# Two branches on one core: first projections in column halves, first weights in longer pieces, and a new order of all steps

## The chip, the cores and the metric

The kernel runs on one core of a Trainium2 chip. A core has a matrix engine (TensorE, in the profile PE, with its weight loads as PEld), VectorE (DVE), ScalarE (ACT), GpSimd (POOL) and SyncE (SP), which here only issues DMA transfers. They run side by side and wait for each other through semaphores. Matrix products land in PSUM, which the kernel uses as eight banks of 128 rows of 512 single-precision numbers. DVE and ACT evict them from there to SBUF, the working memory. The metric is the time of one execution in microseconds on the device; lower is better.

## The reference

Two independent branches read inputs of 2048 tokens by 448 and their outputs are put side by side. Branch A is attention with 16 heads of 28 over 8 keys at distances 0, 2, ... 14:

```python
qkv = x @ wqkv                                   # 448 -> 3 * 448
idx = pos[:, None] - off[None, :]                # off = 0, 2, ..., 14
logits = einsum("bhsd,bhswd->bhsw", q, k[idx]) * 28 ** -0.5
attn = softmax(where(idx >= 0, logits, -1e9))
a = einsum("bhsw,bhswd->bhsd", attn, v[idx]) @ wo
```

Branch B is a linear recurrence with 448 complex states:

```python
Lam_bar = exp(dt * Lam);  B_bar = ((Lam_bar - 1) / Lam)[:, None] * B
h[t] = Lam_bar * h[t - 1] + B_bar @ x[t]
y = 2 * real(C @ h) + x * Dskip
```

## The kernel before, in words

The whole kernel is written out by hand as a list of named steps, the string ORDER (lines 32 to 61). Each word names a function, its arguments as digits, the PSUM banks it takes after "@", and for an eviction the engine: "." is ACT, "=" is DVE. The loop at line 981 runs through the list, and every engine takes its own instructions in the order in which the list emits them. Waits between engines follow from the data. The transfers at lines 149 to 189 are issued ahead of the list, and SP takes them in that order too; what the list sends to SP comes behind them. POOL's constants (lines 193 to 238) are also ahead of the list.

The steps, in the order in which they matter:

- WU (22 products of zeros, L277) and WF (two each, L284) keep PE busy until data is there.
- XI, XH, XA transpose tokens of branch A on PE (L305 to L340); xi, xh, xa copy them from PSUM into xT, in four blocks of columns of x (the fourth, half as wide, comes by XI2 and XH). XI0 and XI1 take tokens 0 to 255 and 256 to 511. The second 1024 tokens are transposed by DMA (L183).
- QS (L374, L375) and QK (L259, the helper `part`) project to q and k for a block m of 128 columns; QK with k = 1 works on 64 rows, in pairs. qk and qh evict them. V_ and v do the same for the values.
- P (L405, DVE) multiplies q by shifted k, 24 of full rows and 4 of half heads, for the halves u = 0 and 1 of the tokens; the results lie in seven buffers used in turn. E_ (L417, L421) sums them over the 28 numbers of each head with products into two banks. lt and TD scale and transpose the scores; sma, smb, smc are the softmax.
- AL, al, ad, sp, AX, adx, spx bring the probabilities into banded form by way of memory (pd, pdx) into PT, 12 slots of a tile each, which pm0 to pm2 clear before on POOL; pm4 clears two of the buffers (Ak) that al2 and al3 fill, pm3 clears wo. AV and av multiply by the values, W_, w and ow are the output projection.
- PP, pcopy, pa to pg compute the constants of branch B; ty, tk, tf, ts make its rotation tables; rb makes small rotations R.
- LC loads C, ci and CD rearrange it, ca and cs scale it. BD and xt transpose B and x by DMA; LD loads Dskip, xd multiplies it.
- BU (L259) is B_bar x for group g of 64 states, BR (L761) adds the step before, z evicts; UP, y, sa, sb, sd, DN, dn carry the recurrence over blocks of four tokens. H_, h, sw, hp (ACT, L872, L874), hy and hz (DVE, L878, L883) bring the carried state back into Z. C, c, oc and, for the last, CH, ch, oh give the output.

xbuf holds x of branch A first, then the transposed x of branch B, then results, so its later uses wait for the earlier ones. The seven P buffers, Cn and Cr lie in memory that PT and wo take over later. The first four weight transfers (w_load at lines 155 and 156) fetch columns 0 to 255 of q and of k in two blocks of 128 columns each, in pieces of 256 bytes.

Of the kernel before, what the change touches and what calls it, by code (L numbers as in the profile page):

```python
# [29 lines left out]


ORDER = """
WU@0 XI0@1 WF0 xi00= xi01= XI2@2 PP@3 pcopy pa XI1@4 WF1 WF2 WF3 xi10. xi20= pb pd_ pc pe xi11. QS00@5 QS10@6 QS30@7
XH1@0 ty0 ty1 pf tk0= tk1= tf0 XA10@1 xh1= QS20@3 pg ab rb0 ts00 xa10. XA11@2 xa11. QK050@40 qk000. xt0 qk010. P000
qk020. QS11@1 qk011. P001 mz QS01@2 qk001. qk030. ts10 P010 ts20 ty4 QS21@5 QS31@6 qk031. qk021. QK041@31 tk4= QK051
P011 V_101@27 QK040 V_100 wj. QK060@65 ty5 qk041. qk040. qk051. v101. V_000@13 qk050. V_011@07 QK061 V_001 v100.
qh011. P020 E_00@42 v000. v001. P021 E_02 tk5= tf2 qh010. P030 qh001. qh000. E_01 P031 P040 P041 P050 P051 V_010
V_400@13 hc0 P060 v011. v010. QK110@56 ts02 ts12 V_401 QK101@70 QK111 E_03 P061 qk110. qk111. QK100 qk100. QK120@56
E_04 qk101. ts22 E_05 E_06 lt00 lt01 QK131@70 QK121 v401. qk120. TD0 QK130 qk130. v400. QK150@42 QK151 QK141@35
QK161@71 qk131. qk150. P100 P101 P110 qk121. qk151. E_10@03 P111 P120 QK140 qk141. P121 QK160 qk140. V_110@46 V_501@25  # L40
qh110. ty2 V_111 P130 P131 qh111. v110. qh101. qh100. v111. E_11 E_12 V_500 V_410@14 V_510@76 V_411 V_511 ty3 BD0 hc1
sma0 smb0 E_13 P140 v500. v501. P141 P150 P151 E_14 E_15 v511. v510. xt2 xt3 xt1 BU300@25 v410. v411. P160 P161 LC
E_16 lt11 BD1 lt10 TD1 smc0 OZ BU301 z30. ci1. LD BU001@67 BU101@14 BU000 ci3. z00. BR31 BU100 BU201@30 z10. AL0@2
al0. z31. BR01 ci0= CD3 CD0 z01. rb3 tk2= BU200 z20. BR11 z11. dk. ci2= CD2 BU011@61 CD1 OP pm3 AL1@2 BR21 BU010 BR02
sma1 z21. BU110@57 smb1 z02. ad0 tk3= tf1 ts01 al1= ad1 BU111 BR03 BR12 xd0 BU210@34 z03. pm4 smc1 BU311@02 z12. ts11
xd1 BU501@65 UP0 BU211 y0= pm0 BR13 BU310 ca3 ca6 z13= wo UP1 cs3 BR32 AX@1 y1= ax. BU500 xd2 ca1 cs6 BU400@71 z50.
ts21 BR51 BR22 AL2@6 BU401 z32. z22. sp0 BU601@03 BR33 sa0 BR23 al2. ty6 BU600 z33. cs1 UP3 z40. z51. sb0 AL3@6 tk6=
tf3 BR41 z23. UP2 BU511@75 z60. y3. BU510 BR61 BU411@02 sd0 y2= ca2 ca4 z41. z61. DN0@4 pm1 sp1 BU410 ts03 ad2 BR52
z52. adx BR42 ts13 z42. BR53 al3= ad3 z53. sa2 dn0 pm2 cs4 AV021@6 av021. AV000@1 AV031@4 AV030@3 UP5 sb2 sd2 av031.
BR43 z43. sp2 AV010@7 av010= y5= AV011@0 DN1@6 av030. dn1 av011. spx AV001@4 AV020@3 DN2@7 dn2 cs2 hp020 UP4 av020.  # L50
DN3@0 av000. BU610@56 dn3 BU611 BR62 W_10@7 W_20@3 y4= ca5 ca0 av001= z62. sa4 H_01@1 h01 sb4 W_00@0 W_01@2 H_00@4
hp012 BR63 W_11@5 hp011 w20. w01. ts23 w11. w10. w00. H_03@1 sd4 W_30@3 W_21@2 DN4@5 z63= hp010 h03 UP6 W_31@7 y6. dn4
hp022 h00 sa6 H_02@0 w21. DN5@1 sp3 AV120@5 av120. dn5 h02 AV111@6 av111. AV131@4 AV121@2 av121. av131. sw2 ow20
AV101@5 av101. AV100@1 H_04@6 cs5 AV130@0 H_05@2 av130. AV110@4 hp123 av110. av100. w30= W_61@3 W_71@5 hp113 cs0 sb6
sd6 C32@0 DN6@4 xd3 ow01 hp025 dn6 C33@1 ow11 sw0 hp111 sw4 hp115 hp122 hp112 ow00 H_06@4 h04 w31= ow31 w71= ow10 ow21
sw6 h05 hp023 hy2 h06 ow30 hp121 C30@6 C31@7 c30 hp021 hz2 hy1 W_51@5 c31 c32 hp124 c33 oc33 C00@2 hp125 C01@4 W_50@6
oc30 oc32 hp013 hy3 W_60@7 hp114 W_40@0 w61. hz1 hp110 hp120 hy0 hp015 hy5 w51. w50= hz5 hz0 hp024 hp014 hy4 C02@3
ow71 hp116 hz3 hz4 hp026 hp016 oc31 hp126 hy6 hz6 W_41@1 w41. w60. ow61 ow50 C03@5 c00 oc00 w40. W_70@6 C12@1 C10@7
C11@0 C13@2 c01 c02 c03 ow41 ow51 oc03 C21@4 oc02 ow40 oc01 w70. C20@6 ow70 c10 c11 c12 oc10 ow60 C22@3 oc11 CH0@5
CH1@7 oc12 c13 c20 c21 oc13 c22 ch0 ch1 oc20 oc21 oc22 oh0 oh1  # L60
"""

@with_exitstack
def kernel(
# [63 lines left out]
    def w_load(c, n, *at):  # L128

        for d in at:  # L130
            SP.dma_start(wq[:, 0:3, c + d:c + d + n], wq_r[:, :, c + d:c + d + n])
# [102 lines left out]
    kph = const.tile([128, 2, 5, G], F32, tag="kph")  # L234
    for k in range(5):
        POOL.memset(kph[:, 0, k], max(k, 1) / (2.0 * T))
    POOL.memset(kph[:, 1], 0.0)
    POOL.memset(kph[64:128, 1, 1:5], 0.25)
# [129 lines left out]
    @op  # L368
    def QS(m, s):

        p = ps()
        pp.setdefault(("qk", 0, m), {})[s] = p
        for kt in range(3):
            PE.matmul(p[:], wqk(m, slice(0, 128), kt), xT[:, 0, 4 * s + kt], start=(kt == 0), stop=False)  # L374
# [641 lines left out]
```

## Time and profile before

| | |
|---|---|
| median of 3 runs | 127.11 us (126.85 to 127.17) |
| the profiled execution | 127.13 us, span 125.4 us |
| busy: PE, DVE, ACT, POOL | 120.6, 113.6, 102.4, 22.7 us |
| instructions: PE, DVE, ACT | 1061, 211, 198 |
| moved by DMA | 22.34 MB, 57493 packets, 43943 of them under 512 B |

The span runs from the first to the last instruction in the trace; the time of the execution holds 1.7 us more that lie around it. Times in the trace are counted from the start of the span. Busy PE time counts overlapping matrix products once; one product of 512 columns lasts 380 ns by itself, but the next one starts about 215 ns after it. In lists by time, a row has its start, its length, engine, line, operation, output and inputs, sizes, the count of merged instructions, and in brackets the idle time of the engine before it with what ended it.

### The profile page before, as it was taken

Reading aid. Unit: us, or ns where it says so; the run is one execution under the profiler, and the core shown is the slowest. Engines: PE = TensorE matmul, PEld = TensorE weight load, DVE = VectorE, ACT = ScalarE, POOL = GpSimd, SP = SyncE. Lnnn points to the kernel's source line nnn. Section 1 sums busy time; section 2 is a strip of 40 time slices with the busy share of each in tenths; the row PEclk is TensorE's granted clock in tenths of the full one; section 3 lists DMA queues with packets and bytes.
Section 4 is the critical chain, followed back from the end, with each engine's and each line's share of the span. In section 5 each row is a group of like instructions: output and inputs, shape, how many; then the busy total and the mean of one; then the engine's idle time right before and its main releaser. Section 6 shows DMA issues by size and latency. Waiting matters only on the chain.

```text
span 125.4 us, 2898 instructions
## 1 busy us (share of the span) xinstructions
PE 120.6 (96%) x1061; PEld 59.0 (47%) x1061; DVE 113.6 (91%) x211; ACT 102.4 (82%) x198; POOL 22.7 (18%) x49
## 2 busy tenths in 40 slices
PE   6999999999999999999999998999999999999990
PEld 6835434443334343344344443745565555555560
DVE  4588999899999999999999999999999999998561
ACT  0599899897596999889999999999999999980000
POOL 6815400000000000090599900000000000000000
PEclk9999999999999999999999999999999999999999
DMA  3898998899969999858999999979854051334652
GB/s 97 208 278 204 325 251 181 191 194 253 157 143 213 204 204 224 144 127 188 358 221 129 160 154 400 156 100 160 177 130 120 0 169 54 124 103 141 227 180 74
DMA packets 57493, 22.34 MB, mean 178 GB/s; under 512 B 43943, under 2 KB 56935, under 8 KB 57479
## 3 DMA queue, kind: packets, MB, share of 16 engines
q1 hardware_dynamic: 57272, 22.08, 82.6%
q8 instruction: 8, 0.13, 0.5%
q10 hardware_dynamic: 207, 0.07, 0.3%
q14 instruction: 6, 0.05, 0.2%
HBM read 9.86 MB, written 6.37 MB: 129 GB/s over the span
## 4 chain that ended last, share of the span: by engine, by line
PE 77%; ACT 17%; DVE 2%; issue 2%; ACTq 0%; DVEq 0%
PE ps L259 27%; PE ps L897 16%; PE ps L573 10%; ACT Z L114 7%; ACT ctmp L722 5%; PE ps L417 5%; PE ps L374 4%; PE ps L560 4%; PE ps L277 2%; PE ps L827 1%; PE ps L375 1%; PE ps L922 1%; PE ps L761 1%; ACT L694 1%; PE ps L421 1%
## 5 line engine op out<-in xcount | busy, mean ns | idle before, releaser
L405 DVE TENSOR_TENSOR pr<-qf,kf 128x2048 bf16<-128x2048 bf16 x24 | 27.9, 1220 | 0.7 <-PE ps L417 0.4
L259 PE MATMUL ps<-xbuf,BT 128*128 128x512 bf16 (+1 forms) x112 | 25.1, 380 | 0.0
L897 PE MATMUL ps<-Cw,Z 128*128 128x448 bf16 x105 | 20.9, 352 | 0.0
L259 PE MATMUL ps<-xT,wq 128*128 128x512 bf16 (+1 forms) x72 | 16.0, 380 | 0.0
L259 PEld LDWEIGHTS <-BT 128*128 128x128 bf16 (+1 forms) x112 | 9.1, 96 | 12.9 <-issue 4.5
L897 PEld LDWEIGHTS <-Z 128*128 128x128 bf16 x105 | 10.3, 98 | 9.5 <-DVE Z L883 0.2
L114 ACT CAST Z<-ps 128x512 bf16<-128x512 f32 (+1 forms) x28 | 13.8, 547 | 0.2
L573 PE MATMUL ps<-wo,oT 128*128 128x448 bf16 x64 | 13.7, 353 | 0.0
L259 PE MATMUL ps<-wq,xT 128*128 128x448 bf16 (+1 forms) x64 | 12.3, 353 | 0.0
L973 POOL MEMSET PT<- 128x4320 f32 x3 | 11.0, 3698 | 4.7 <-DVE z L461 4.7
L259 PEld LDWEIGHTS <-wq 128*128 128x128 bf16 (+1 forms) x72 | 5.9, 97 | 8.6 <-issue 2.4
L722 ACT ACTIVATE ctmp<-Cw,c2t 64x448 f32<-64x448 bf16 x14 | 9.3, 666 | 0.2
L573 PEld LDWEIGHTS <-oT 128*128 128x128 bf16 x64 | 6.2, 98 | 5.7
L259 PEld LDWEIGHTS <-xT 128*128 128x128 bf16 (+1 forms) x64 | 5.2, 97 | 6.8 <-issue 2.4
L114 ACT CAST qf<-ps 128x512 bf16<-128x512 f32 x12 | 6.8, 594 | 1.8 <-PE ps L259 1.5
L114 ACT CAST oT<-ps 128x512 bf16<-128x512 f32 x15 | 8.1, 641 | 0.0
L114 ACT CAST v_s<-ps 128x448 bf16<-128x448 f32 x16 | 7.9, 548 | 0.0
L761 PE MATMUL ps<-Z,R 128*128 128x512 bf16 x21 | 7.3, 381 | 0.5 <-ACT Z L114 0.5
L114 ACT CAST kf<-ps 128x512 bf16<-128x512 f32 x12 | 7.1, 604 | 0.3 <-PE ps L375 0.2
L949 POOL MEMSET Z<- 128x14 bf16 x1 | 0.1, 111 | 38.9 <-ACT Cn L117 38.9
L374 PE MATMUL ps<-xT,wq 128*128 128x512 bf16 x24 | 6.6, 379 | 0.3 <-DVE u L627 0.2
L872 ACT ACTIVATE PT<-PT,bcol 128x512 bf16<-128x512 bf16 x8 | 6.3, 816 | 0.0
(172 smaller groups left out, 226.8 us busy)
## 6 DMA issues: line engine op xcount, KB each, us to landing
PT<-pd SPq DMA_DIRECT2D x16, 156.0 KB, 4.8
...
```

The lines of the kernel that those rows point to most:

```text
L114: (ACT.copy if e == "A" else V.tensor_copy)(o, i)
L259: PE.matmul(o, l, r, start=(first and i == 0), stop=(not first and i == len(pairs) - 1 and not more[s]))
L374: PE.matmul(p[:], wqk(m, slice(0, 128), kt), xT[:, 0, 4 * s + kt], start=(kt == 0), stop=False)
L405: V.tensor_tensor(t[:], q.unsqueeze(1).to_broadcast((128, 4, 512)), k4, ALU.mult)
L417: PE.matmul(acc[s][32 * i:32 * i + 32], E[:, f, ws, :], t[:, i, :], start=(f == 0 and ws == 0), stop=False)
L560: PE.matmul(p[32 * hh:32 * hh + 32, 128 * bl:128 * bl + n], v_s[:, t, 4 * hg + hh, :], PT[:, t % NS, (4 * hg + hh) // HS, (4 * hg + hh) % ...
L573: PE.matmul(p[:, 0:D], late["oT"][:, b // 4, hg, par, 128 * (b % 4):128 * (b % 4) + 128], late["wo"][:, hg, :], start=(hg == 0), stop=(hg ...
L722: ACT.activation(t[a:a + 64, 0:D], Cw[b:b + 64, g, :], ACTF.Copy, scale=c2t[a:a + 64, g:g + 1])
L761: PE.matmul(pp["z", g, j][:], rot(g, 0), late["Z"][:, g, j - 1, :], start=False, stop=True)
L872: ACT.activation(t, late["SW"][:, NC * g:NC * (g + 1)], ACTF.Copy, scale=bcol[:, j - 1, g:g + 1])
L897: PE.matmul(p[:, 0:D], z, Cw[:, g, :], start=(g == 0), stop=(g == G - 1))
L973: POOL.memset(late["PT"][:, 4 * i:4 * i + 4].rearrange("p t g n -> p (t g n)").bitcast(F32), 0.0)
```

## The change

1. The first four weight transfers become two: columns 0 to 255 of q and of k in one each, in pieces of 512 bytes.
2. A new step QA(m, a) projects block m for half a (256 columns of tokens) of the first 512 tokens. QA(0, 1), QA(0, 0), QA(1, 0) and QA(1, 1) take the place of QS00 and QS10.
3. On POOL, the constants kph are set before the halos and masks, and so is the row of numbers iota, which was set before them already and now follows kph.
4. WF4 is added: two more products of zeros.
5. All steps stand in a new order, with other banks; 18 evictions or table steps go from ACT to DVE and 22 from DVE to ACT. LC goes from behind the score steps to the start of the list, so its four loads are the first that the list sends to SP.

```diff
 ORDER = """
-WU@0 XI0@1 WF0 xi00= xi01= XI2@2 PP@3 pcopy pa XI1@4 WF1 WF2 WF3 xi10. xi20= pb pd_ pc pe xi11. QS00@5 QS10@6 QS30@7
-XH1@0 ty0 ty1 pf tk0= tk1= tf0 XA10@1 xh1= QS20@3 pg ab rb0 ts00 xa10. XA11@2 xa11. QK050@40 qk000. xt0 qk010. P000
-qk020. QS11@1 qk011. P001 mz QS01@2 qk001. qk030. ts10 P010 ts20 ty4 QS21@5 QS31@6 qk031. qk021. QK041@31 tk4= QK051
-P011 V_101@27 QK040 V_100 wj. QK060@65 ty5 qk041. qk040. qk051. v101. V_000@13 qk050. V_011@07 QK061 V_001 v100.
-qh011. P020 E_00@42 v000. v001. P021 E_02 tk5= tf2 qh010. P030 qh001. qh000. E_01 P031 P040 P041 P050 P051 V_010
-V_400@13 hc0 P060 v011. v010. QK110@56 ts02 ts12 V_401 QK101@70 QK111 E_03 P061 qk110. qk111. QK100 qk100. QK120@56
-E_04 qk101. ts22 E_05 E_06 lt00 lt01 QK131@70 QK121 v401. qk120. TD0 QK130 qk130. v400. QK150@42 QK151 QK141@35
-QK161@71 qk131. qk150. P100 P101 P110 qk121. qk151. E_10@03 P111 P120 QK140 qk141. P121 QK160 qk140. V_110@46 V_501@25
-qh110. ty2 V_111 P130 P131 qh111. v110. qh101. qh100. v111. E_11 E_12 V_500 V_410@14 V_510@76 V_411 V_511 ty3 BD0 hc1
-sma0 smb0 E_13 P140 v500. v501. P141 P150 P151 E_14 E_15 v511. v510. xt2 xt3 xt1 BU300@25 v410. v411. P160 P161 LC
-E_16 lt11 BD1 lt10 TD1 smc0 OZ BU301 z30. ci1. LD BU001@67 BU101@14 BU000 ci3. z00. BR31 BU100 BU201@30 z10. AL0@2
-al0. z31. BR01 ci0= CD3 CD0 z01. rb3 tk2= BU200 z20. BR11 z11. dk. ci2= CD2 BU011@61 CD1 OP pm3 AL1@2 BR21 BU010 BR02
-sma1 z21. BU110@57 smb1 z02. ad0 tk3= tf1 ts01 al1= ad1 BU111 BR03 BR12 xd0 BU210@34 z03. pm4 smc1 BU311@02 z12. ts11
-xd1 BU501@65 UP0 BU211 y0= pm0 BR13 BU310 ca3 ca6 z13= wo UP1 cs3 BR32 AX@1 y1= ax. BU500 xd2 ca1 cs6 BU400@71 z50.
-ts21 BR51 BR22 AL2@6 BU401 z32. z22. sp0 BU601@03 BR33 sa0 BR23 al2. ty6 BU600 z33. cs1 UP3 z40. z51. sb0 AL3@6 tk6=
-tf3 BR41 z23. UP2 BU511@75 z60. y3. BU510 BR61 BU411@02 sd0 y2= ca2 ca4 z41. z61. DN0@4 pm1 sp1 BU410 ts03 ad2 BR52
...
+WU@0 XI0@1 xi00. LC PP@2 pcopy pa XI2@3 pb xi20. pc WF0 XI1@4 WF1 WF2 xi10= xi01= WF3 xi11= pe WF4 pf pd_ tk1= QA01@5
+tk0. QA00 qk000. QA10@6 QS30@7 XH1@2 xh1. XA10@3 xa10. QA11 XA11@0 xa11. QS20@1 pg rb3 rb0 qk010. wj. QS01@4 ty1
+QS11@5 QK041@23 ty0 QK061@06 qk011. QK060 qk001. qk030. qk020. P000 P001 tf0 qh001. qh011. qh000. xt1 ts00 QK040
+qk041. QS21@5 QS31@4 P010 P011 P020 qk021. qk031. QK050@71 V_011@03 qk040. qh010. QK051 ts10 V_101@54 qk050. tk4.
+E_00@26 P021 E_02 ts20 hc0 P030 E_01 V_010 v011. qk051. V_100 QK100@73 ty4 v010. ty5 P031 P040 tk5. QK101 qk100.
+QK111@10 E_03 P041 P050 QK110 qk101. P051 tf2 P060 v100. QK130@73 mz ts02 qk110. v101. tk3. E_04 E_05 qk111. P061 E_06
+ts12 tk2. ts22 QK141@51 QK131 qk131. qk130. lt00 QK121@40 QK120 qk120. ty2 BD0 QK140 QK150@37 lt01 TD0 qk121. qk140.
+QK161@24 P100 P101 P110 P111 qk141. ci3. QK151 qk151. qk150. V_411@60 P120 P121 P130 ty3 E_10@53 E_12 QK160 qh110.
+P131 P140 V_000@17 qh111. xt3 qh101. qh100. V_410 v410. v411. E_11 P141 P150 xt2 xt0 E_13 V_111@42 V_001 ci2. v000.
+sma0 v001. hc1 V_511@60 P151 P160 LD P161 ci0= CD3 V_510 v510. V_500@17 V_110 V_501 tf1 v511. V_401@60 smb0 ci1. ab
+E_14 smc0 E_15 E_16 lt10 lt11 v501. v110. tk6. CD2 v111. V_400 v401. dk. TD1 BU100@53 BU000@74 xd2 v400. CD0 BU001 BD1
+CD1 BU101 BU111@20 AL1@6 sma1 OZ OP pm3 z00. z10. al1. ad1 AL0@7 BR01 BR11 z11= v500. al0. BU200@56 BU110 smb1 BR12
+z01= ts01 smc1 BU301@17 BU201 BU011@34 BU010 z20= BU300 z12. z30= ts11 BR02 BR13 ca3 cs3 BR21 BU500@25 z02= BU501 ca6
+ca1 xd0 z13. z21. BU211@13 BR03 z03. z50. BU210 BR22 ts21 xd1 UP1 y1. ad0 BR31 pm0 cs1 AL2@6 wo sp0 z22= UP0 y0. cs6
+BR51 BR23 z51. pm1 sa0 BU400@21 pm4 z23. UP2 al2. sp1 AL3@0 AX@4 y2= BU310@56 BU311 z31. BU401 BU511@73 ca2 ca4 sb0
+BR32 z32. BU510 ax= adx ad2 al3. BR33 sd0 DN1@4 BR52 cs4 cs2 DN0@5 dn0 z40. BR41 z33. UP3 y3= pm2 ad3 z52. sp2 ca5 dn1
...
 """
...
-    w_load(0, 128, 0, D)
-    w_load(128, 128, 0, D)
+    w_load(0, 256, 0, D)
...
+    @op
+    def QA(m, a):
+        first = ("qa", m) not in begun
+        begun.add(("qa", m))
+        if first:
+            pp.setdefault(("qk", 0, m), {})[0] = ps()
+        p, c = pp["qk", 0, m][0], slice(256 * a, 256 * a + 256)
+        for kt in range(3):
+            PE.matmul(p[:, c], wqk(m, slice(0, 128), kt), xT[:, 0, kt, c], start=(first and kt == 0), stop=False, skip_group_check=True)
+        PE.matmul(p[:, c], wzz[:, 0, m % 2, 64 * (m - m % 2):64 * (m - m % 2) + 128], xT[:, 0, 3, c], start=False,
+                  stop=(not first), skip_group_check=True)
```

In the part of the list that is cut, both orders run the steps AV, W_, H_, hp, hy, hz and C, c with their neighbours; the new one starts the block of eight AV with B = 1 in one piece, and ends with hz6, w60, w40, w70, xd3 and then C00, C01, C02, C13 and so on.

More of the change, by code (lines that the diff above doesn't have):

```diff
@@ L48 @@
-tf3 BR41 z23. UP2 BU511@75 z60. y3. BU510 BR61 BU411@02 sd0 y2= ca2 ca4 z41. z61. DN0@4 pm1 sp1 BU410 ts03 ad2 BR52
[L49 to L57, printed above, removed]
@@ L58 @@
-ow71 hp116 hz3 hz4 hp026 hp016 oc31 hp126 hy6 hz6 W_41@1 w41. w60. ow61 ow50 C03@5 c00 oc00 w40. W_70@6 C12@1 C10@7
-C11@0 C13@2 c01 c02 c03 ow41 ow51 oc03 C21@4 oc02 ow40 oc01 w70. C20@6 ow70 c10 c11 c12 oc10 ow60 C22@3 oc11 CH0@5
-CH1@7 oc12 c13 c20 c21 oc13 c22 ch0 ch1 oc20 oc21 oc22 oh0 oh1
+WU@0 XI0@1 xi00. LC PP@2 pcopy pa XI2@3 pb xi20. pc WF0 XI1@4 WF1 WF2 xi10= xi01= WF3 xi11= pe WF4 pf pd_ tk1= QA01@5
+tk0. QA00 qk000. QA10@6 QS30@7 XH1@2 xh1. XA10@3 xa10. QA11 XA11@0 xa11. QS20@1 pg rb3 rb0 qk010. wj. QS01@4 ty1
@@ new lines @@
+z01= ts01 smc1 BU301@17 BU201 BU011@34 BU010 z20= BU300 z12. z30= ts11 BR02 BR13 ca3 cs3 BR21 BU500@25 z02= BU501 ca6
+ca1 xd0 z13. z21. BU211@13 BR03 z03. z50. BU210 BR22 ts21 xd1 UP1 y1. ad0 BR31 pm0 cs1 AL2@6 wo sp0 z22= UP0 y0. cs6
+BR51 BR23 z51. pm1 sa0 BU400@21 pm4 z23. UP2 al2. sp1 AL3@0 AX@4 y2= BU310@56 BU311 z31. BU401 BU511@73 ca2 ca4 sb0
+BR32 z32. BU510 ax= adx ad2 al3. BR33 sd0 DN1@4 BR52 cs4 cs2 DN0@5 dn0 z40. BR41 z33. UP3 y3= pm2 ad3 z52. sp2 ca5 dn1
+sa2 z41. ty6 BU600@02 tf3 BR53 z53. BU411@75 BU601 AV000@6 AV030@4 av030. H_00@1 BU410 sb2 z60. BR61 h00 H_01@4 h01
@@ new lines @@
+ts03 av000. z61. UP5 y5. BR42 AV001@0 AV010@6 sd2 AV031@1 z42. av010. AV021@2 av021. AV020@3 AV011@4 av020= spx hp010
+BR43 z43. av001. av031= BU610@76 UP4 DN2@2 av011. y4= ts13 ca0 DN3@3 dn3 BU611 BR62 z62. W_11@0 W_20@1 dn2 W_01@4
+hp012 sa4 hp020 w20. ts23 sp3 w01. BR63 z63. cs5 sb4 H_03@5 h03 sw0 sd4 w11. W_10@3 W_00@2 H_02@7 ow01 W_21@1 w10.
+ow10 hp011 UP6 y6= h02 W_31@4 AV130@5 w00. w21= ow20 ow00 av130. AV111@0 av111. AV100@3 AV120@2 AV110@6 av120. av110=
+AV131@5 av131= av100. AV121@7 AV101@0 av121. ow11 ow21 sa6 W_30@1 DN5@2 W_60@6 DN4@3 sw2 av101. dn4 w30= sb6 W_71@7
@@ new lines @@
+w31. ow31 W_50@5 hp110 hp121 hp023 dn5 hp021 W_41@0 W_61@4 H_05@3 W_51@1 sd6 cs0 ow30 H_04@2 sw4 w71. hp120 w61= w51=
+DN6@7 ow71 dn6 w50. C33@5 hy0 ow50 ow61 H_06@4 h05 w41. hp013 hz0 h04 ow41 ow51 C31@0 hp022 hp122 h06 hp111 hy1 hp124
+hp025 sw6 hp115 hp112 C30@1 c30 hy2 c31 C32@7 c32 hp015 oc31 hp125 hy5 hp123 C03@3 hz1 W_40@2 hp024 hp113 hz5 hp014
+W_70@4 hp114 hp016 hp126 oc30 hz2 hp026 hy4 hy3 hz4 hp116 hz3 hy6 oc32 hz6 w60. w40. w70. xd3 ow70 ow60 C00@1 c33
+C01@0 c00 c01 C02@7 c02 C13@6 C11@2 C10@4 oc33 C12@5 c03 c10 c11 oc01 C21@1 C20@0 oc00 ow40 C22@7 CH0@3 oc10 oc03 oc02
@@ L61 @@
+CH1@4 c12 oc12 c13 c20 oc13 oc11 c21 c22 ch0 oc20 oc21 oc22 oh0 ch1 oh1
 """
@@ L194 @@
     iot = const.tile([128, N2], F32, tag="iota")
-    POOL.iota(iot[:], [[1, N2]], base=0, channel_multiplier=0, allow_small_or_imprecise_dtypes=True)
     cols = const.tile([128, 6], F32, tag="cols")
@@ L202 @@
         POOL.memset(col[64:128], hi)
+    kph = const.tile([128, 2, 5, G], F32, tag="kph")
+    for k in range(5):
+        POOL.memset(kph[:, 0, k], max(k, 1) / (2.0 * T))
+    POOL.memset(kph[:, 1], 0.0)
+    POOL.memset(kph[64:128, 1, 1:5], 0.25)
+    POOL.iota(iot[:], [[1, N2]], base=0, channel_multiplier=0, allow_small_or_imprecise_dtypes=True)
     kf = s1.tile([128, 3, HALO + S], BF16, tag="kf")
@@ L232 @@
                        channel_multiplier=-1)
[L234 to L238, printed above, removed]
     wq6 = s2.tile([128, 4, 2, 64], BF16, tag="wq6")
```

## The prediction

> **What bounds the kernel now.** I read the page first (busy shares, the chain that ended last), then the busy time by stretches, then the waits, then the timelines of the front and the tail.
>
> ```profile
> PE 120.6 (96%) x1061; PEld 59.0 (47%) x1061; DVE 113.6 (91%) x211; ACT 102.4 (82%) x198; POOL 22.7 (18%) x49
> ...
> PE 77%; ACT 17%; DVE 2%; issue 2%; ACTq 0%; DVEq 0%
> ```
> ```profile
> core 0: us, PE busy (x) PEld busy (x) DVE busy (x) ACT busy (x) POOL busy (x), PEclk, DMA share, GB/s
> 50.50:70.00 19.50, 19.50 (x140) 8.57 (x141) 19.03 (x32) 18.88 (x34) 12.26 (x7) 1.00 0.85 193
> 84.00:112.70 28.70, 28.70 (x297) 15.39 (x295) 28.29 (x61) 28.43 (x53) 0.00 (x0) 1.00 0.52 116
> ```
> ```profile
> PEld L259 <- issue: 9.8, 25, 0.4
> ```
>
> The chain is PE for 77%. In the stretches (busy time of each engine, first the length) PE is full, and DVE and ACT are within 0.6 us of full from 50.5 to 112.7: three engines run out together. The last row (weight loads that wait for nothing the profile shows) comes in below. The tail shows it:
>
> ```profile
> 109.91 0.79 ACT L872 ACTIVATE PT<-PT,bcol 128x512 bf16<-128x512 bf16 x1
> 111.99 0.69 DVE L883 TENSOR_TENSOR Z<-Z,PT 128x1024 bf16<-128x1024 bf16 x1
> 111.70 9.43 PE L897 MATMUL ps<-Cw,Z 128*128 128x448 bf16 x49
> 120.97 1.50 PE L922 MATMUL ps<-Cw,Z 128*128 128x224 bf16 x14
> ```
>
> hz6 (L883) ends at 112.68, and the seventh product of C12, begun at 111.70, wants its result after six products of 0.19 each, at 112.85. After that 9.6 us of products remain, whatever came before. So a gain must reach PE, hp/hy/hz on ACT and DVE, all three.
>
> **The front.** Before:
>
> ```profile
> 1.82 2.33 SPq L131 DMA_DIRECT2D wq<-in_A_wqkv_dram  x4
> 3.49 0.82 PE L309 MATMUL ps<-ident,xbuf 128*128 128x128 bf16 x6
> 4.35 0.62 DVE L114 COPY xT<-ps 128x512 bf16<-128x512 bf16 x2 [1.77 <-PE ps L309]
> 6.39 0.60 ACT L617 ACTIVATE rk<-are 128x7 f32<-128x7 f32 x5
> 6.89 0.36 ACT L114 COPY xT<-ps 128x256 bf16<-128x256 bf16 x1
> 7.30 0.38 PE L374 MATMUL ps<-xT,wq 128*128 128x512 bf16 x1 [0.16 <-DVE u L627]
> 8.60 0.81 PE L374 MATMUL ps<-xT,wq 128*128 128x512 bf16 x3
> ```
>
> QS00's third product starts at 7.30 (the row marked with a wait), 0.05 after xi11 ended on ACT behind the five exponentials; the page's name for that wait (DVE, 0.16) is not the cause. QS30 follows at 8.60. After the change XI0 (6 x 0.10 from 3.49), PP (0.18), XI2 (0.43, its rows are there by 4.3) and WF0 (0.21) bring XI1 to 4.92, and by its row's 0.82 it ends near 5.75. DVE, now free of xi00 and xi20, then copies xi10, xi01, xi11: 0.42 and 0.28 for the two old copies of 4.35, 0.28 for the third, until 6.62 with their small gaps. ACT does xi00 and xi20 instead; it copied 128 rows in 0.59 where DVE took 0.43, so they cost it 0.4 to 0.6 each, in time in which it waited for P (1.01 in the old front). The two added zero products (0.21) only fill PE until 6.40, in the shadow of xi11; without that cover they would cost 0.21. QA01 and QA00 and QA10 are twelve products of 256 columns. The nearest row for such a product is L773, 0.11 between starts; so 1.3 us plus 0.05 of waiting, and QS30 begins near 7.75 instead of 8.60. QA11 (0.43) is still to come: **-0.42**. If the four extra weight loads (0.10 each) are not hidden it is 0; if nothing waits, -0.6. I take -0.42, as L773 lies nearest.
>
> ```profile
> 1.80:3.40 1.60, 1.60 (x17) 1.51 (x15) 0.63 (x3) 0.53 (x1) 1.23 (x11) 1.00 0.84 247
> 3.40:5.40 2.00, 2.00 (x21) 1.70 (x20) 0.83 (x4) 0.98 (x3) 1.69 (x8) 1.00 0.92 213
> 72.84 0.27 PE L773 MATMUL ps<-Z,R 128*128 128x256 bf16 x1
> ```
>
> The pieces: 393 KB move at 213 GB/s while 256-byte pieces flow and x's longer ones moved at 247, so 0.25 us is to be had on the transfer, and two issues (1.16 of SP's 2.33) go. I count nothing for it, since xi11 ends last, not the weights. The Trainium skill (DMA: Bandwidth & Descriptors, Specifications) says that transfers under 512 bytes miss line rate; by that rule, if the weights were last, the sum would be 0.25 lower.
>
> **Moved issues and constants.** LC's four loads now stand in SP's queue before xt1, BD0, TD0 and the other xt:
>
> ```profile
> 34.48 1.23 SPq L439 DMA_TRANSPOSE attn<-lt  x1
> 37.77 6.37 SPq L734 DMA_TRANSPOSE xbuf<-xnB  x3
> 44.20 1.09 SPq L289 DMA_DIRECT2D Cr<-in_B_C_re_dram  x1
> 46.53 0.51 SPq L290 DMA_DIRECT2D Cr<-in_B_C_im_dram  x1
> ```
>
> They take 2.83 (44.20 to 47.04), 1.16 is won ahead, so what follows is 1.7 late; TD0's wait before 34.48 takes part of that up, as BD0 now goes ahead of it. With three xt in 6.37 after TD0 the last xt is issued by about 43.4, its first reader (BU100) comes near 50; TD0 ends near 37, sma0 reads it after 43. Hidden. If LC's own landing is late, ci3 (ACT) waits some 0.3, with 0.4 behind it free. The kph memsets ahead of the masks let pe run before pd_, and ACT can fetch the sine's table while it waits for pe, not after; the masks come about 0.5 later and are first read after 19 us. With pg earlier (8.75 for 10.34) and rb3 (1.08) put before it, the first P starts near 12.35 on DVE, before at 13.08.
>
> **The score stage, where the new order pays.**
>
> ```profile
> 22.66 1.48 PE L417 MATMUL ps<-pr,E 128*32 128x512 bf16 x24
> 23.11 5.77 DVE L405 TENSOR_TENSOR pr<-qf,kf 128x2048 bf16<-128x2048 bf16 x5 [0.40 <-PE ps L417]
> 40.45 0.28 DVE L445 TENSOR_TENSOR attn<-attn,mk 128x256 bf16<-128x256 bf16 x1
> 42.42 4.62 DVE L405 TENSOR_TENSOR pr<-qf,kf 128x2048 bf16<-128x2048 bf16 x4
> 46.97 2.35 DVE L405 TENSOR_TENSOR pr<-qh_t,kh 128x2048 bf16<-128x2048 bf16 x2
> ```
>
> A P costs DVE 1.14 (42.42 to 46.97 over four). Twenty-eight of them (31.9), two tf (1.2 together) and sma0 (1.97, from 40.45 to the next P at 42.42) are 35.2 with the last one's end, so P161 would end at 47.6. The products have seven buffers; P141 reuses P110's, which E_11 reads, and E_11 now stands behind QK160, V_000 and V_410, at about 40.35. A buffer comes free 0.45 after its E starts (22.66 to 23.11), so P141 waits from 39.85 to 40.8: P161 ends at 48.6 (before 49.32). PE, laid end to end in the new order, would want it at 46.25: E_06, E_12, V_500 and above all E_16 wait **+2.4** in sum. The next product starts at 48.95. This is the largest price, and it follows from three fewer microseconds of PE work ahead of the same DVE work.
>
> **After E_16.** Here PE wins.
>
> ```profile
> 33.24 0.60 PE L259 MATMUL ps<-xT,wzz 64*128 64x512 bf16 x4
> 33.78 3.52 PE L259 MATMUL ps<-xT,wq 128*128 128x512 bf16 x18
> 69.44 0.99 PE L259 MATMUL ps<-xbuf,BT 64*128 64x512 bf16 x4
> 70.37 0.61 PE L761 MATMUL ps<-Z,R 128*128 128x512 bf16 x2
> 76.72 0.59 PE L761 MATMUL ps<-Z,R 128*128 128x512 bf16 x2
> 77.86 0.38 PE L761 MATMUL ps<-Z,R 128*128 128x512 bf16 x1 [0.54 <-ACT Z L114]
> ```
>
> Four 64-row products run in pairs, 0.43, yet the next full one starts 0.54 later: a change of shape costs PE 0.10, and of the 25 weight-load gaps named "issue" most are these. Counted along the old list there are 54 changes, along the new 39; after E_16 32 and 18: **-1.4**. The Trainium skill (TensorEngine Tiling (Array Packing), Key Properties) says that a change of tiling mode drains the array and a change of tile within a mode does not; counted by that rule it is the same 54 and 39.
>
> Two real waits of the old order go, one after 64-row products and one after full ones: 69.44 to 70.37 is 0.93 where 0.53 is due, and 77.86 is 0.6 late; with a small one that makes **-1.05** if nothing replaces them. Before, PE needed 71.85 from E_16's end (50.43) to its last product's end by pace (122.28). New: plus V_400 and BU300 moved behind E_16 (2.45), less 1.45 and 1.05, is 71.8; from 48.95 that gives 120.75, **1.5 earlier**.
>
> ACT and DVE must follow.
>
> ```profile
> 50.57 1.09 ACT L430 ACTIVATE lt<-ps 128x512 bf16<-128x512 f32 x2 [0.51 <-PE ps L421]
> ```
>
> From the second lt (ends 51.66) to the last hp (110.70) ACT needed 59.0 with hardly a gap. The new list has 0.75 less there (eighteen steps gone to DVE, twenty come), from 50.25: 108.5, plus waits of about 1.2 (al2 on POOL, smb1 on sma1, the second AV block). That is 109.75, and hy6, hz6 end 1.4 later (two DVE steps of 0.68), 111.15; before 112.68. DVE has 1.35 less between P161 and hz6: 48.6 + 63.36 - 1.35 = 110.6. PE and ACT say 1.5 earlier, DVE 2.1, so it is not the last.
>
> I give back 0.6 for small waits: the old order has 1.05 of them in the same stretch, and in the new one bank releases and their readers lie 0 to 0.5 apart almost everywhere from AL1 to W_11. Sum: -1.5 + 0.6 = **-0.9**. The profiled span is 125.4 in a run of 127.13 (1.7 outside it), and the median of the runs is 127.11: 126.2.
>
> **Rivals.**
>
> ```profile
> 47.08 2.93 SPq L710 DMA_TRANSPOSE BT<-Bn  x1
> 53.82 5.23 SPq L715 DMA_TRANSPOSE Cw<-Cn  x4
> 53.89 1.16 POOL L969 MEMSET oT<- 128x1280 f32 x1
> 60.89 10.98 POOL L973 MEMSET PT<- 128x4320 f32 x3 [4.74 <-DVE z L461]
> ```
>
> *Slower: ACT stopped by POOL at al2.* pm4's two memsets (1.16 each) came before pm0's wait; now they stand behind pm0 and pm1 (3.66 each), and al2 writes what pm4 clears. pm0 started 1.85 after the last CD was issued (59.04). (The page names smc1's first step, which was under way then; of the four waits at that place I take the transpose's landing. By smc1's step pm0 would come at 58.4, half a microsecond sooner.) In the new queue TD1 (1.23), CD0 (1.3), BD1 (2.93), CD1 (1.3) follow lt11: CD1 is issued by 57.0, pm4 ends at 68.5, and ACT wants al2 at 68.1. The 0.4 is in my sum. But if CD1 is no earlier than the old last one, al2 waits 2.35, and z31, ca2, ca4, z32 and BR33 behind it: 126.2 + 2.0 = 128.2. It turns the sign once CD1 is 0.9 later than I put it. For it: DMA transposes took 1.24 to 2.93 each. Against: by then LC is long done.
>
> *No change: the small waits are not 0.6 but 1.5.* Each is under 0.5; but nothing behind E_16 has slack to take them. 127.1.
>
> *The front brings nothing*, since the weights still land at the old time: QS30 at 8.2; but P161 then ends on DVE's chain as before, and the end is 126.4. It is inside the forecast.
>
> **Numbers.** Forecast (faster, 125.4 to 126.7): 0.57. No change, within 0.3% (about what this measurement can tell from none): 0.14. Slower: 0.29, of which al2 0.17 and other late data (PT's last transfer before the second AV block, 0.7 of margin) 0.12. Low end: 1.5 without the give-back, and the front at its lower bound, 0.2 less: 125.4. High end: the al2 case, 128.2.
>
> **What would show it.** QS30 near 7.75 and the first P near 12.35; a DVE wait on PE of about 0.95 at the P before sma0; weight loads on E waiting for DVE, the longest at E_16; fewer "issue" gaps of 0.4; hz6 near 111.2. Wrong if ACT waits for POOL at L114 with more than a microsecond, if AV waits for PT, or if P161 ends after 49.3.

## The result and the profile after

The changed kernel takes 125.67 us (median of 20 runs, 125.64 to 127.32) where the kernel before takes 127.10 beside it: a ratio of 0.991, with a 95% interval of 0.989 to 0.994. Four of the twenty runs took 127.3 us at a granted clock of 0.985 instead of 1.00; they widen the interval and don't move the median. The profiled execution has a span of 124.0 us, before 125.4. The forecast was 126.2, so the gain is 1.4 instead of 0.9. The sum came near the end, but several of its terms were wrong and one stall was missing from it, as the trace shows stage by stage.

First the page of the changed kernel (busy time, and the chain that ended last), then its busy time in the stretches asked of before, and its waits.

```profile
PE 117.2 (95%) x1061; PEld 58.8 (47%) x1071; DVE 114.0 (92%) x207; ACT 103.8 (84%) x202; POOL 22.7 (18%) x49
```
```profile
50.50:70.00 19.50, 19.29 (x153) 9.28 (x156) 19.03 (x32) 19.12 (x38) 12.64 (x7) 1.00 0.88 192
82.50:111.20 28.70, 28.70 (x302) 15.65 (x300) 28.29 (x61) 27.91 (x52) 0.00 (x0) 1.00 0.52 120
```
```profile
PEld L258 <- issue: 7.6, 19, 0.4
...
ACT sc L646 <- DVE u L642: 1.9, 1, 1.9
PE ps L386 <- ACT xT L114: 1.9, 1, 1.9
```

PE, DVE and ACT still run out together (the second stretch is moved by 1.5, as the end is). The weight loads that wait for nothing the profile shows fell from 25 to 19, as the smaller count of shape changes lets expect. The two waits of 1.9 are new, and no step of the prediction has them. They lie in the front. Here are the rows of POOL, DVE, ACT and PE from the timeline of that stretch, and last the same step k in the kernel before:

```profile
6.86 2.23 POOL L683 MEMSET Ak<- 128x2560 f32 x1
```
```profile
6.66 0.30 DVE L640 TENSOR_TENSOR u<-u,kph 128x35 f32<-128x35 f32 x1
7.00 2.13 DVE L641 TENSOR_SCALAR k<-u 128x35 f32<-128x35 f32 x1
9.16 0.20 DVE L642 SCALAR_TENSOR_TENSOR u<-k,u 128x35 f32<-128x35 f32 x1
...
13.96 1.22 DVE L417 TENSOR_TENSOR pr<-qf,kf 128x2048 bf16<-128x2048 bf16 x1
```
```profile
9.39 0.23 ACT L646 ACTIVATE sc<-u 128x35 f32<-128x35 f32 x1 [1.88 <-DVE u L642]
...
11.24 2.10 ACT L114 COPY xT<-ps 64x512 bf16<-64x512 bf16 x3
```
```profile
7.99 0.59 PE L373 MATMUL ps<-xT,wq 128*128 128x512 bf16 x2
...
11.88 0.27 PE L386 MATMUL ps<-xT,wzz 128*128 128x256 bf16 x1 [1.85 <-ACT xT L114]
```
```profile
7.63 0.18 DVE L629 TENSOR_SCALAR k<-u 128x35 f32<-128x35 f32 x1
```

The step k (L641) of 35 numbers a row takes 2.13 us, where it took 0.18 before, and ends at 9.13, 0.04 after the memset mz on POOL (6.86 to 9.09). The new list sends mz to POOL much later in the text than the old one, but it has moved ab, which stood ahead of mz in POOL's queue, further still. ab waits for pg on DVE; without it ahead, mz runs as soon as POOL is done with the masks. Then the sine on ACT waits for k, the copy xh1 (the first of the three at 11.24) for the sine, QA11 on PE for xh1, and the first P starts at 13.96 instead of the forecast 12.35.

From there on the stages stand as follows. The rows are from DVE's timeline (the P around sma0, and the last P), from PE's (E_11, the first row here, and the last products), and from DVE's and ACT's tail (hz6, hp116).

```profile
37.88 5.76 DVE L417 TENSOR_TENSOR pr<-qf,kf 128x2048 bf16<-128x2048 bf16 x5
43.56 0.28 DVE L457 TENSOR_TENSOR attn<-attn,mk 128x256 bf16<-128x256 bf16 x1
...
46.73 2.35 DVE L417 TENSOR_TENSOR pr<-qh_t,kh 128x2048 bf16<-128x2048 bf16 x2
```
```profile
42.36 1.05 PE L429 MATMUL ps<-pr,E 128*32 128x512 bf16 x16
...
49.54 1.31 PE L258 MATMUL ps<-wq,xT 128*128 128x448 bf16 x6
...
119.37 1.50 PE L934 MATMUL ps<-Cw,Z 128*128 128x224 bf16 x14
```
```profile
110.20 0.69 DVE L895 TENSOR_TENSOR Z<-Z,PT 128x1024 bf16<-128x1024 bf16 x1
```
```profile
108.55 0.74 ACT L884 ACTIVATE PT<-PT,bcol 128x512 bf16<-128x512 bf16 x1
```

P161 ends at 49.08, the first product behind E_16 (V_400) starts at 49.54, hz6 ends at 110.89 and the last product at 120.87.

### The profile page after: what moved, and what is told of

Same layout as the page of the kernel before. It is cut to its first block, busy times and chain, and to the rows that moved or that the text cites. A ratio compares the mean times of both kernels' runs of the same rounds, so it can differ in the third digit from the quotient of the medians.

```text
span 124.0 us, 2908 instructions
## 1 busy us (share of the span) xinstructions
PE 117.2 (95%) x1061; PEld 58.8 (47%) x1071; DVE 114.0 (92%) x207; ACT 103.8 (84%) x202; POOL 22.7 (18%) x49
## 4 chain that ended last, share of the span: by engine, by line
PE 91%; DVE 3%; ACT 2%; issue 1%; DVEq 0%
PE ps L258 39%; PE ps L909 16%; PE ps L585 10%; PE ps L429 5%; PE ps L773 4%; PE ps L572 4%; PE ps L373 3%; PE ps L276 2%; DVE k L641 2%; PE ps L839 1%; PE ps L934 1%; PE ps L499 1%; PE ps L433 1%; PE ps L374 1%; PE ps L308 1%
## 5 line engine op out<-in xcount | busy, mean ns | idle before, releaser
L258 PE MATMUL ps<-xbuf,BT 128*128 128x512 bf16 (+1 forms) x107 | 23.1, 379 | 0.3
L909 PE MATMUL ps<-Cw,Z 128*128 128x448 bf16 x105 | 20.3, 352 | 0.0
L258 PE MATMUL ps<-xT,wq 128*128 128x512 bf16 (+1 forms) x69 | 15.5, 380 | 0.3 <-issue 0.2
L114 ACT CAST Z<-ps 128x512 bf16<-128x512 f32 (+1 forms) x25 | 11.7, 516 | 0.1
L114 ACT CAST oT<-ps 128x512 bf16<-128x512 f32 x13 | 7.1, 616 | 0.1
L114 ACT CAST ya<-ps 128x448 bf16<-128x448 f32 (+1 forms) x13 | 6.8, 565 | 0.0
L429 PE MATMUL ps<-pr,E 128*32 128x512 bf16 x96 | 6.3, 382 | 0.0
```

The lines of the kernel that those rows point to most:

```text
L114: (ACT.copy if e == "A" else V.tensor_copy)(o, i)
L258: PE.matmul(o, l, r, start=(first and i == 0), stop=(not first and i == len(pairs) - 1 and not more[s]))
L429: PE.matmul(acc[s][32 * i:32 * i + 32], E[:, f, ws, :], t[:, i, :], start=(f == 0 and ws == 0), stop=False)
L909: PE.matmul(p[:, 0:D], z, Cw[:, g, :], start=(g == 0), stop=(g == G - 1))
```

## The experiments

Theory 1 at the start: mz ahead of ab stops DVE and costs the front; the rest of the gain comes from fewer shape changes and from waits that are gone. Rival: the front is not on the path, and the loads, the constants and the halves bring what there is.

**ab ahead of mz.** In POOL's queue only; all else as in the changed kernel.

```diff
-QS20@1 pg rb3 rb0 qk010.
+QS20@1 pg ab rb3 rb0 qk010.
...
-smb0 ci1. ab
-E_14
+smb0 ci1. E_14
```

> The changed kernel with one step moved in POOL's queue: ab (which waits for DVE) ahead of mz (the memset of Ak, 2.23 us), as it was in the old order. Theory 1, POOL's memset stops DVE: in the changed kernel the step at L641 took 2.13 us while that memset ran (6.86 to 9.09), so now it takes about 0.2, the first P starts near 12.3 instead of 13.96, and PE's wait of 1.85 before QA11's last product goes. As P141 then waits for E_11's buffer, only part comes through: P161 ends near 48.6 instead of 49.1, and the time falls by 0.2 to 0.6 us, to about 125.3. Theory 2, the step was slow for another reason (its own operands): L641 stays at 2.1 and nothing moves. Theory 3, the block is gone but the end is set behind E_16 alone: first P near 12.3, time the same, 125.7.

It takes 124.27 us (124.02 to 124.57), a ratio to the kernel before of 0.977 (0.976 to 0.979): 1.4 faster than the changed kernel, where 0.2 to 0.6 was expected. In the timeline of this kernel's front mz runs behind ab, k takes 0.36, and the first P starts at 12.22:

```profile
9.72 2.22 POOL L682 MEMSET Ak<- 128x2560 f32 x1
```
```profile
6.58 0.36 DVE L640 TENSOR_SCALAR k<-u 128x35 f32<-128x35 f32 x1
...
9.77 2.09 DVE L714 TENSOR_TENSOR R<-Is,co 128x896 bf16<-128x896 bf16 x2
12.22 2.36 DVE L416 TENSOR_TENSOR pr<-qf,kf 128x2048 bf16<-128x2048 bf16 x2 [0.36 <-ACT kf L113]
...
45.00 2.35 DVE L416 TENSOR_TENSOR pr<-qh_t,kh 128x2048 bf16<-128x2048 bf16 x2
```
```profile
118.25 1.50 PE L933 MATMUL ps<-Cw,Z 128*128 128x224 bf16 x14
```

The memset now lies over rb3 and rb0 (9.77, two steps on two tensors), and these are not slowed: 2.09 for two, as in the changed kernel. P161 ends at 47.36, 1.72 earlier, V_400 starts at 47.99, 1.55 earlier, and the last product (PE's last row) ends at 119.75, 1.12 earlier. So the stall was on the path for the most part; the 0.46 that is lost behind V_400 is a new wait at BU100, which comes up again below.

**mz ahead of ab in the kernel before.**

```diff
-QS20@3 pg ab rb0
+QS20@3 mz pg ab rb0
...
-P001 mz QS01@2
+P001 QS01@2
```

> The old kernel with mz moved ahead of ab in POOL's queue, nothing else. Theory 1 (POOL's memset stops some DVE steps): the memset runs from about 6.9 to 9.1, a step of DVE on one tensor (L623, L629 or a tensor_scalar near them) takes until about 9.1 instead of 0.2, the first P moves from 13.08 to about 14.5, and since DVE and PE are both full in the old order the time rises by 0.5 to 1.5 us, to about 128. Theory 2 (the slow step in the changed kernel has another cause): 127.1, no DVE step above 0.6 in the front.

129.03 us (129.02 to 129.07), 1.9 slower than the kernel before, where 0.5 to 1.5 was expected: the same stall in the old order, and the first P starts at 14.97 instead of 13.08. In DVE's timeline two steps end together with the memset on POOL; the second, on two tensors, is queued behind the first:

```profile
6.84 2.23 POOL L671 MEMSET Ak<- 128x2560 f32 x1
```
```profile
6.95 2.15 DVE L623 TENSOR_SCALAR fT<-fT,cols 128x7 f32<-128x7 f32 x1
7.09 2.01 DVE L627 TENSOR_TENSOR u<-f,kph 128x35 f32<-128x35 f32 x1
```

**The same steps on two tensors.** The changed kernel with mz still first; k, km and fT are computed by steps that read a second tensor and give the same values.

```diff
-V.tensor_scalar(k4[:], u4[:], MAGIC, None, ALU.add)
+V.scalar_tensor_tensor(k4[:], u4[:], MAGIC, kph[:, 0], ALU.add, ALU.max)
-V.tensor_scalar(km[:], f8[:], MAGIC, None, ALU.add)
+V.scalar_tensor_tensor(km[:], f8[:], MAGIC, f8[:], ALU.add, ALU.max)
-V.tensor_scalar(fT[:], fT[:], way, None, ALU.mult)
+V.scalar_tensor_tensor(fT[:], fT[:], way, kph[:, 1, 0], ALU.mult, ALU.add)
```

> The changed kernel itself, mz still ahead of ab, but the three DVE steps on one tensor in pe and pd_ (k = u + M, km = f + M, fT times way) written as steps on two tensors with the same values. Theory 1: only steps on one single-precision tensor in SBUF stand still under a memset on POOL, so k takes 0.2 to 0.4 instead of 2.13, QA11 no longer waits, and the time is that of the kernel with ab ahead of mz, 124.3 (123.9 to 124.6). Rival: any single-precision DVE step from SBUF stands still under the memset: k still ends at 9.1, 125.7.

124.73 us (124.15 to 125.04), ratio 0.979 (0.977 to 0.982): two thirds of the gain of the other queue order, without changing the queue. POOL's and DVE's timelines show which steps the memset stops:

```profile
6.94 2.23 POOL L683 MEMSET Ak<- 128x2560 f32 x1
```
```profile
6.67 0.37 DVE L641 SCALAR_TENSOR_TENSOR k<-u,kph 128x35 f32<-128x35 f32 x1
...
7.58 0.23 DVE L635 SCALAR_TENSOR_TENSOR fT<-fT,cols,kph 128x7 f32<-128x7 f32 x1
...
8.65 0.54 DVE L656 TENSOR_SCALAR ab<-ab 128x7 f32<-128x7 f32 x1
```

Steps on two tensors under the memset run at their usual pace; L656, the one step on one tensor that was left, stands until 9.19, when the memset ends (9.17). In the changed kernel it takes 0.19. The clean pair is fT, 7 numbers a row: 2.15 as a step on one tensor under the memset (the run before this one), 0.23 here on two. So it is the form of the step that counts, not its size. (k itself starts before the memset in this run.) Of the 0.46 that is missing, L656 is no part as far as the trace tells: DVE waits 0.36 for ACT ahead of the first P afterwards. The first P comes 0.38 later than with ab first since weights and rows of x came later in the profiled run (XH1, which waits for x, starts at 9.46 instead of 9.09).

POOL's mask selects, which read a tensor where a memset reads none, stop steps on two tensors as well. From POOL's and DVE's timelines of the kernel with QA11 earlier (the experiment that follows):

```profile
6.01 0.53 POOL L231 TENSOR_SCALAR_AFFINE_SELECT mk<-m 128x256 bf16<-128x256 bf16 x1
```
```profile
6.12 0.43 DVE L638 TENSOR_TENSOR u<-f,kph 128x35 f32<-128x35 f32 x1
```

L638 takes 0.18 with ab first, where it starts ahead of the select; here it ends at 6.55, 0.01 behind it. This is read from the traces; no run was made for it. The k of 0.36 with ab first (one tensor) and of 0.37 in the kernel with two tensors end in the same way, 0.03 and 0.04 behind the second select.

**Whole columns again, and QA11 earlier.** Both stand on the kernel with ab first. The first puts QS00 and QS10 back; the second keeps the halves and moves QA11 ahead of XH1, which waits for x.

```diff
 # whole columns
-QA01@5 tk0. QA00 qk000. QA10@6 QS30@7 XH1@2 xh1. XA10@3 xa10. QA11 XA11@0
+QS00@5 tk0. qk000. QS10@6 QS30@7 XH1@2 xh1. XA10@3 xa10. XA11@0
 # QA11 earlier
-QA10@6 QS30@7 XH1@2 xh1. XA10@3 xa10. QA11 XA11@0
+QA10@6 QS30@7 QA11 XH1@2 xh1. XA10@3 xa10. XA11@0
```

> The kernel with ab ahead of mz, with QS00 and QS10 in whole columns again in place of the four QA. Theory 1, the prediction's: the halves are what brings QS30 forward by 0.42, so without them the end is 0.4 later, 124.7. Theory 2: in that kernel QA01 starts at 6.06, when the last of the three copies ends, as a whole QS00 would, and XH1 waits 0.53 for its rows of x until 9.09 whatever stands ahead of it; QA11 (0.44) then lies ahead of that wait instead of behind it, so XA10 and all that follows comes 0.4 earlier: 123.9.

> The kernel with ab ahead of mz, with QA11 moved from behind XA10 to behind QS30, halves kept. Theory 2 (the halves bring nothing, QA11 fills the wait for x): XH1 still starts at 9.09, XA11 at 9.72 instead of 10.16, the end 0.3 to 0.44 earlier, 123.9, the same as with whole columns. Theory 1: the halves bring 0.42 over whole columns, so this kernel is 0.4 or more faster than that one. If the first P waits for something else than PE's products, no change: 124.3.

124.18 us (123.81 to 124.46) and 124.35 (124.13 to 124.62), beside 124.27: no difference that these runs can tell. Both theories miss; the third case, that the first P waits for something else than PE's products, fits. QS30 starts at 7.80 with halves and at 8.30 with whole columns, and the first P at 12.22 and 12.30. The halves bring nothing, and filling the wait for x brings nothing either, since PE then waits for ACT two steps later. From the timelines of PE and ACT in the kernel with QA11 earlier:

```profile
11.05 0.86 PE L372 MATMUL ps<-xT,wq 128*128 128x512 bf16 x3 [0.34 <-ACT xT L113]
```
```profile
8.77 0.59 ACT L113 CAST qf<-ps 128x512 bf16<-128x512 f32 x1
9.38 2.11 ACT L113 COPY xT<-ps 64x512 bf16<-64x512 bf16 x3
11.37 0.60 ACT L113 CAST kf<-ps 128x512 bf16<-128x512 f32 x1
```

ACT copies without a gap from 8.77 on, and DVE, with pg, rb3 and rb0, is not free before 12.08. These two set the first P, not PE. The three kernels with ab first, 124.2 to 124.4 us against 127.1 before, are the fastest of this study.

**The loads.** Once in the kernel before (weights in two transfers and constants first, nothing else), once the other way round in the kernel with ab first (four transfers of 256-byte pieces).

```diff
 # in the kernel before
-    w_load(0, 128, 0, D)
-    w_load(128, 128, 0, D)
+    w_load(0, 256, 0, D)
 # in the kernel with ab first
-    w_load(0, 256, 0, D)
+    w_load(0, 128, 0, D)
+    w_load(128, 128, 0, D)
```

> The old kernel with only the first weights in two transfers of 512-byte pieces and the constants kph ahead of the masks; the list of steps is the old one. Theory 1, the front is bound by the copies of xT and not by the weights: QS00's third product still at about 7.3, time 127.1 within 0.2. Theory 2, the weights' landing matters: QS00 to QS30 up to 0.4 earlier and a time of about 126.7.

> The kernel with ab ahead of mz, with the first weights in four transfers of 256-byte pieces as before. Theory 1, the prediction's (the transfers bring nothing, since the copies end last): 124.3, QA01 at 6.06, within 0.1. Rival: the rows of x behind them in SP's queue are issued 1.16 later, XH1 waits for them (0.53 now) and starts up to 1.1 later; the end 0.5 to 1.1 later, 124.8 to 125.4.

In the old order 127.45 us (126.81 to 127.68), ratio 1.002 (1.0005 to 1.0035): no gain, and QS00's third product starts at 7.37 (7.30 before). In the new order with four transfers 124.56 (124.38 to 124.94), ratio 0.979 (0.977 to 0.982), against 0.977 (0.976 to 0.979) with two; the intervals overlap, and two transfers are worth 0 to 0.3 us. The front does get later with four, by more than that: QS30 waits for weights (PE's timeline), and the first P starts at 12.91.

```profile
8.53 0.59 PE L373 MATMUL ps<-xT,wq 128*128 128x512 bf16 x2 [0.70 <-DMA wq<-in_A_wqkv_dram]
```

E_16's first weight load comes at 48.03, against 47.43 with two transfers, but BU100's comes at 49.55 and 49.56. The weight loads of the kernel with two, and its products, show why:

```profile
47.98 0.87 PEld L257 LDWEIGHTS <-xT 128*128 128x128 bf16 x6 [0.42 <-issue]
49.56 1.85 PEld L257 LDWEIGHTS <-BT 128*128 128x128 bf16 x10 [0.71 <-issue]
```
```profile
47.99 1.31 PE L257 MATMUL ps<-wq,xT 128*128 128x448 bf16 x6
49.60 2.10 PE L257 MATMUL ps<-xbuf,BT 128*128 128x512 bf16 x9 [0.30 <-issue]
```

V_400's six products start 0.19 apart, so BU100's first could start 1.15 after V_400's, as it does in the changed kernel (49.54 and 50.69) and with four transfers (48.59 and 49.73). Here it starts 1.61 after, 0.46 late. BU100 reads the transposed x, whose last transfer lands at 49.39 there; with whole columns it lands at 49.02 and BU100 loads at 49.19, with QA11 earlier at 49.17 and 49.34. So BU100 comes 0.17 behind that landing in all three. In the changed kernel the same transfer landed at 46.42 and BU100 did not wait. That this is the next bound is read from the traces; it was not tried.

**The price of a shape change.** First by six more of them in the changed kernel (BU300 ahead of BU201, BR32 ahead of BU401, AL1 ahead of BU111: 45 for 39).

```diff
-BU101 BU111@20 AL1@6
+BU101 AL1@6 BU111@20
...
-BU301@17 BU201 BU011@34 BU010 z20= BU300
+BU301@17 BU300 BU201 BU011@34 BU010 z20=
...
-BU311 z31. BU401 BU511@73 ca2 ca4 sb0 BR32 z32.
+BU311 z31. BR32 BU401 BU511@73 ca2 ca4 sb0 z32.
```

> The changed kernel with three products of branch B moved by a step or two (BU300 before BU201, BR32 before BU401, AL1 before BU111), so that PE changes the shape of its products 45 times instead of 39; the same work, the same banks. Theory 1, a change of shape costs PE 0.10 and PE has no slack behind E_16: +0.6 us, 126.3, and the weight loads show six more gaps named issue. Theory 2, the changes are hidden behind waits for ACT and DVE: within 0.2 of 125.7.

126.37 us (126.32 to 126.44): 0.70 more than the changed kernel, 0.12 for each. The gaps named issue at the weight loads rise by five, not by the six expected (four at the helper's line, one at AL's). But moved steps can also move waits. So, second, the price by itself: in the kernel with ab first, each of the 15 steps C of the tail, where PE waits for nothing, gets one short product of zeros more in its middle, once on 128 rows, once on 64. The output stays the same.

```diff
 # in C(j, ct), behind the product of g == 3
+PE.matmul(p[:, D:512], wz[0:128, :], wz[0:128, 0:64], start=False, stop=False, skip_group_check=True)
 # or
+PE.matmul(p[:, D:512], wz[0:64, :], wz[0:64, 0:64], start=False, stop=False, skip_group_check=True)
```

> The kernel with ab ahead of mz, with one more product of zeros (128 rows, 64 columns) into the free columns of the bank in the middle of each of the 15 steps C, which PE runs with nothing else to wait for. No change of shape is added. Both theories: 15 short products at 0.05 to 0.11 each, 0.8 to 1.6 more, 125.0 to 125.9.

> The same with the added product on 64 rows instead of 128: 30 changes of shape more, and nothing else. Theory 1, the prediction's (a change costs PE 0.10): 3.0 later than with 128 rows. Rival: the 0.10 belongs to the waits and copies around the old pairs, and a change by itself costs nothing: the same as with 128 rows, within 0.3.

125.33 us (124.81 to 125.85) with full rows, 128.19 (127.93 to 128.9) with 64: 2.86 us for 30 changes, **0.095 each**; the scatter of these runs, about 1 us, leaves some 0.013 either way. The waits view of the kernel with 64 rows has a line that the other lacks:

```profile
PEld L910 <- issue: 5.6, 15, 0.4
```

Fifteen gaps of 0.37 at the added product's weight load (5.6 over 15), the kind that was read as a shape change in the prediction.

These runs price changes between 128 and 64 rows. Counted in the two traces, only 6 of the 15 changes that the new order saves are of that kind; the other 9 lie between products that use 128 columns of the array and 32 (128\*128 and 128\*32 in the rows). No run adds such a change, but PE's timeline of the changed kernel shows its price where AV follows a product of 512 columns:

```profile
78.78 0.38 PE L773 MATMUL ps<-Z,R 128*128 128x512 bf16 x1
79.08 1.71 PE L572 MATMUL ps<-PT,v_s 128*32 128x135 bf16 x96
```

AV starts 0.30 after that product, where the next one of the same shape starts 0.215 after: the same 0.09 to 0.1.

**CD1 later.** In the kernel with ab first, CD1, and with it OP and pm3, behind both ad in SP's queue (ad0 is moved ahead for it): this makes the case of the slower rival.

```diff
-CD1 BU101 BU111@20 AL1@6 sma1 OZ OP pm3 z00. z10. al1. ad1 AL0@7 BR01 BR11 z11= v500. al0. BU200@56
+BU101 BU111@20 AL1@6 sma1 OZ z00. z10. al1. ad1 AL0@7 BR01 BR11 z11= v500. al0. ad0 CD1 OP pm3 BU200@56
...
-UP1 y1. ad0 BR31
+UP1 y1. BR31
```

> The kernel with ab ahead of mz, with CD1 put behind both ad in SP's queue, so that the last transpose out of Cn is issued 1.5 to 1.9 later (at 54.20 now) and pm0 and with it pm4 follow. al2 starts on ACT at 66.97 now, 0.01 after the last memset of pm4 ended on POOL. The prediction's rival (ACT stopped by POOL at al2): pm4 ends at 68.2 to 68.8, ACT waits 1.2 to 1.9 there, and the end is 1.0 to 1.9 later, 125.3 to 126.2. If POOL waits for something else (BD1's landing, at 56.43 now), or ACT's delay is made up behind it, no change: 124.3.

126.89 us (126.66 to 127.85), ratio to before 0.999 (0.9975 to 1.0005): the whole gain is lost as far as the runs can tell, 2.6 us, where 1.0 to 1.9 was expected. First two rows of POOL's timeline with CD1 in its old place, then POOL's and ACT's with CD1 later:

```profile
57.41 7.34 POOL L984 MEMSET PT<- 128x4320 f32 x2
64.69 1.17 POOL L980 MEMSET oT<- 128x1280 f32 x1
```
```profile
61.45 7.34 POOL L984 MEMSET PT<- 128x4320 f32 x2 [4.20 <-DMA wo<-in_A_wo_dram]
68.73 1.17 POOL L980 MEMSET oT<- 128x1280 f32 x1
```
```profile
61.12 4.07 ACT L733 ACTIVATE ctmp<-Cw,c2t 64x448 f32<-64x448 bf16 x6 [1.73 <-DMA Cw<-Cn]
...
69.93 0.59 ACT L113 CAST oT<-ps 128x512 bf16<-128x512 f32 x1 [1.18 <-POOL oT L980]
```

pm0 starts 4.0 later, though CD1 is issued only 1.7 later (55.89 for 54.20); why it lands so late, 5.2 after its issue, stays open. al2 waits 1.18 for pm4's first memset, which ends at 69.90, as the rival has it. The other part the expectation had left out: ca3 scales what CD1 writes, and waits 1.73 for it. (The page names wo's transfer for POOL's wait. But pm0 clears the memory that CD1 reads, not wo, and CD1's landing at 61.1, by ca3's row, fits.)

The moves of evictions between ACT and DVE, the new banks and WF4 were not run alone; their share in the gain stays open.

## Why the prediction was right, and where not

*The front: wrong term, and a stall that was missing.* QS30 started at 7.99 (7.75 forecast), but that was worth nothing: with whole columns the end is the same. The first P is set by ACT's copies and DVE's rb3 and rb0. Nor did the copies end last alone: with ab first PE waits 0.43 at QA01 for the copies and then 0.20 for weights, with QA11 earlier 0.38 for weights. The position 12.35 for the first P was right for the kernel without the stall (12.22), and the stall made it 13.96. The step that failed is the list of what moves on POOL: it has the constants, kph and pm4, and not mz, which the new order puts ahead of ab. Its price was 1.4 us, as large as the whole gain.

*The score stage: P161.* A P chain of 35.2 from the first P was right: 35.12 in the changed kernel, 35.14 with ab first. The wait of 0.95 for E_11's buffer was wrong: the five P from 37.88 run without a gap until 43.64, and E_11 starts only at 42.36, behind P141's start (41.28). P141 can't use the buffer that E_11 reads. E_12 stands ahead of E_11 in the new list, so its buffers come free first; that P141 takes one of those is concluded, not shown. The two errors, 1.6 too early and 0.95 too late, nearly cancel: P161 ends at 49.08 (48.6 forecast), V_400 starts at 49.54 (48.95). E_06, E_12 and E_16 did not wait for DVE, because PE itself was later than the laying end to end had it: by QA11's 1.85, and by the shape changes ahead of E_16, of which there are 21 (2.0 at 0.095). With ab first the 1.85 is gone, E_16 starts at 47.43 against the 46.25 laid, and still does not wait; the runs don't separate what makes up the 1.2.

*After E_16.* From V_400 to the last product's end it is 71.3 us (49.54 to 120.87), and 71.8 with ab first, of which 0.46 is BU100's wait: the 71.8 worked out was 0.5 too long, with shape changes at 0.10 (0.095 measured alone). The term that is too small is the waits that go: summed from start to start of PE's products, the old order loses about 1.7 in that stretch, not 1.05 (0.7 ahead of 77.86, 0.4 ahead of 70.37, and the rest in small ones up to 0.18). The 0.6 given back for small waits did not come: apart from BU100's, no wait over 0.02 is left there with ab first. Without that give-back the sum would have been -1.5, which is what was measured, but by luck: the stall took 1.4, and 0.95 of P141 and 0.6 of small waits were counted that don't exist.

*ACT and DVE.* hp116 ends at 109.29 (109.75), hz6 at 110.89 (111.15), P161 on DVE as above: none of them ends last, as forecast. (The forecast's count of moved steps, eighteen and twenty, is not the list's, which moves 18 and 22 in all, and 16 and 13 of those that stand behind the second lt in both orders.)

*Moved issues.* In the changed kernel LC's early issue and the constants cost nothing that shows. With ab first BU100 waits 0.46 for the transposed x, which the forecast had as hidden and which LC's loads stand ahead of in SP's queue; a kernel with LC behind it was not run. The two transfers are worth at most 0.3 in the new order and nothing in the old one, as counted.

*The rivals.* al2 needs only the first of pm4's two memsets, as the run with CD1 later shows (it starts 0.03 behind it). In the changed kernel that one ends at 66.69 and the second at 67.80, and al2 starts at 68.07: 1.38 of margin, where the forecast set the end of the second (68.5) against the wish of ACT (68.1) and saw 0.4 of waiting. With pm0 4.0 later al2 does wait, by 1.18. The rival's mechanism holds; its threshold was put too near. "The front brings nothing" described the halves rightly.
